# Another order for the first chunks of a fused retention and maxout kernel

## Chip, cores, metric

One core of one Trainium2 chip. The time is device microseconds (us) of one execution; the profile's "span", from the first to the last instruction, is about 1.7 us shorter than the time of the same execution. The engines are PE (TensorE matmul; PEld its weight loads), DVE (VectorE), ACT (ScalarE), POOL (GpSimd) and SP (SyncE, which here only issues DMAs).

## The reference

```python
# q, k, v: (8 batches, 8 heads, 576, 64) float32; moe_w1..3: 512x768; moe_w_out: 768x512
def _attn_ref(q, k, v):
    scores = matmul(q, k.T) / sqrt(64)
    gamma = 1 - 2.0 ** (-5 - arange(8))                      # one per head
    ret = scores * where(rel >= 0, gamma ** rel, 0)          # rel = row - column, causal decay
    return matmul(ret, v)

def _moe_ref(x, w1, w2, w3, w_out):                          # x: 4608 x 512
    return maximum(maximum(x @ w1, x @ w2), x @ w3) @ w_out

x = attn.transpose(0, 2, 1, 3).reshape(4608, 512)            # tokens by heads*head_dim
```

## The kernel before

The 4608 tokens are worked in 36 chunks of 128 rows, four chunks to a tile of 512, nine tiles. A chunk of attention is: two groups of transposes (kT, qT), scores, DVE's masked scores `st`, values `o` from the chunk itself plus the part from the running state ("old state"), then DVE scales `o` into `xT`, the input of the feed-forward part. The state is kept by DVE (`keep`), from chunk to chunk, and scaled by GpSimd.

The weights arrive as float64 bits. DVE and ACT turn each 128x512 block into float32 in four steps of `convert`: expo, frac (two steps), then mant, then expo again and `w`. The feed-forward part of a tile runs while the next tile's attention is done piecewise in between. Only the first chunks ("the head") have nothing to run beside; they are what the change reorders. Tile 0 uses plain matmuls ("up", "down"); later tiles use a seven-product scheme (x, y, z, S, T in the profile).

```python
P, C = 128, 128; CPT = 4                    # chunks per tile
ps_r = tile_pool(bufs=4, space=PSUM)        # tag "r": scores; o from tile 1 on
ps_x = tile_pool(bufs=2, space=PSUM)        # tag "x"
ps_y = tile_pool(bufs=2, space=PSUM)        # tag "y"
opool = tile_pool(bufs=2)                   # output blocks "osb" on their way to memory
# ... cut

def transposes(g):                          # ... cut
    for n, src in (("k", raws["k", g]), ("q", raws.pop(("q", g)))):
        pool, tag = (ps_r, "r") if g > CPT else (ps_x, "x")
        pt = pool.tile([P, NP, C], FP32, tag=tag, name=n + "t")
        for p in range(NP):
            nc.tensor.transpose(pt[:, p, :], pair(src, p), ident[:C, :C])
        t = both[n] = att.tile([P, NP, C], FP32, tag=n + "T", name=n + "T", bufs=2 if n == "k" else 3)
        nc.scalar.copy(t[:], pt[:])

def scores(g):
    s = [ps_r.tile([C, NP, C], FP32, tag="r", name=f"s{j}") for j in range(2)]
    # ... cut: 16 matmuls of kT and qT
    for j in range(2):
        nc.vector.tensor_tensor(st[:, j], s[j][:], mask, op=ALU.mult)

def state(g):
    kr = raws["k", g]
    if begins(g):
        r = start_of(g) or 0
        pool, tag = (ps_r, "r") if g >= CPT else (ps_x, "x")
        kvs[g] = pool.tile([P, NP, D], FP32, tag=tag, name="kv")
        # ... cut: 8 matmuls of k and vd

def keep(g):
    kv = kvs.pop(g)
    # ... cut: first chunk of a batch
    nc.vector.tensor_tensor(t[:], kv[:], states[g][:], op=ALU.add)
    nc.gpsimd.tensor_tensor(t[:], t[:], gs[:], op=ALU.mult)

def values(chunks, new_states=()):
    t, i = divmod(chunks[0], CPT)
    pool, tag = (ps_r, "r") if t > 0 else (ps_y, "y")
    # ... cut: o from st and vd
    for g in new_states:
        state(g)
    # ... cut: old state: o += states[g] x qT
    # ... cut: two DVE products o * gq into xT
    for g in new_states[:1]:
        keep(g)

def decay_values(g):                        # GpSimd: vd = v * decay
    ...

def downs_plain(t, h):                      # tile 0, ... cut
    osb = opool.tile([P, DM], FP32, tag="osb", name="osb")
    nc.scalar.copy(osb[:], b[:])
    nc.sync.dma_start(out[...], osb[:])     # same queue as all loads of q, k, v and weights

decay_values(0); transposes(0); warm(2)     # warm: matmuls of the identity, result unused
decay_values(1); scores(0); transposes(1); scores(1)
decay_values(2); values([0], [0]); transposes(2); scores(2)
values([1], [1]); decay_values(3); transposes(3); scores(3)
convert(2); values([2], [2]); convert(2); transposes(4)
decay_values(4); convert(2); values([3], [3]); convert(4)
# then, per tile: feed-forward steps with the next tile's attention between them
```

## Time and profile before

| | before |
|---|---|
| time, median of 3 | 800.32 us (800.2 to 800.5) |
| span of the profiled execution | 797.9 us, mean clock 1.000 |
| PE idle in the whole span | 797.9 - 785.7 = 12.2 us |
| PE idle before the first "up" (at 30.59) | 7.84 us |

These are stretches of the kernel before; the columns are start and end, length, busy time of PE, PEld, DVE, ACT and POOL (with instructions), PE's clock, the DMA share and GB/s:

```profile
10.00:20.00 10.00, 8.31 (x128) 6.81 (x128) 4.46 (x10) 2.06 (x4) 2.09 (x2) 1.00 1.02 240
20.00:31.00 11.00, 7.59 (x125) 6.21 (x126) 8.24 (x17) 6.17 (x10) 3.90 (x4) 1.00 0.87 218
31.00:120.00 89.00, 89.00 (x428) 44.81 (x430) 78.36 (x141) 50.80 (x77) 7.45 (x7) 1.00 0.67 161
```

PE has idle time in the head and none from 31 to 120 us. The clock is 1.00 in all three. (The first 10 us have 7.26 us busy.)

### The profile page before, as it was taken

Reading aid. Unit: us, or ns where it says so; the run is one execution under the profiler, and the core shown is the slowest. Engines: PE = TensorE matmul, PEld = TensorE weight load, DVE = VectorE, ACT = ScalarE, POOL = GpSimd, SP = SyncE. Lnnn points to the kernel's source line nnn. Section 1 sums busy time; section 2 is a strip of 40 time slices with the busy share of each in tenths; the row PEclk is TensorE's granted clock in tenths of the full one; section 3 lists DMA queues with packets and bytes.
Section 4 is the critical chain, followed back from the end, with each engine's and each line's share of the span. In section 5 each row is a group of like instructions: output and inputs, shape, how many; then the busy total and the mean of one; then the engine's idle time right before and its main releaser. Section 6 shows DMA issues by size and latency. Waiting matters only on the chain. (4 is left out here: it accounts for less than half of the span.)

```text
span 797.9 us, 13707 instructions
## 1 busy us (share of the span) xinstructions
PE 785.7 (98%) x5128; PEld 642.9 (81%) x5128; DVE 414.4 (52%) x833; ACT 174.2 (22%) x401; POOL 139.5 (17%) x158
## 2 busy tenths in 40 slices
PE   7899999999999999999999999999999999999998
PEld 6545546888888888888888888888888888888887
DVE  2897978664354634363535344544545343642341
ACT  2664642111111102111111111111111111111211
POOL 2210108421210130112211121112111201110000
PEclk9999999999999999999999999999999999999999
DMA  9995644333333332332233333333333333001001
GB/s 216 230 226 123 155 108 102 57 57 57 87 57 57 58 78 55 68 58 61 61 55 57 67 82 57 57 57 89 56 55 58 80 62 59 1 14 40 1 1 53
DMA packets 237506, 59.27 MB, mean 74 GB/s; under 512 B 218240, under 2 KB 236160, under 8 KB 237440
## 3 DMA queue, kind: packets, MB, share of 16 engines
q1 hardware_dynamic: 236176, 58.01, 33.5%
q8 instruction: 40, 0.66, 0.3%
q10 hardware_dynamic: 1264, 0.40, 0.2%
q14 instruction: 26, 0.21, 0.1%
HBM read 48.89 MB, written 9.44 MB: 73 GB/s over the span
## 5 line engine op out<-in xcount | busy, mean ns | idle before, releaser
L493 PE MATMUL x<-S,T 128*128 128x256 f32 x576 | 148.1, 380 | 0.7 <-ACT p L498 0.6
L493 PEld LDWEIGHTS x<-S,T 128*128 128x128 f32 x576 | 108.9, 190 | 16.8 <-ACT p L498 1.5
L343 POOL TENSOR_TENSOR H<-h 128x256 f32<-128x256 f32 x24 | 21.0, 874 | 321.2 <-DVE h L536 321.2
L493 PE MATMUL x<-xT,w 128*128 128x256 f32 x288 | 76.1, 387 | 0.0
L493 PE MATMUL x<-S,w 128*128 128x256 f32 x288 | 74.4, 381 | 0.7 <-DVE h L523 0.7
L493 PE MATMUL z<-S,w 128*128 128x256 f32 x288 | 73.9, 379 | 0.0
L493 PE MATMUL y<-xT,w 128*128 128x256 f32 x288 | 73.9, 379 | 0.0
L493 PE MATMUL z<-xT,T 128*128 128x256 f32 x288 | 73.9, 379 | 0.0
L523 DVE TENSOR_TENSOR tmp<-x,p 128x256 f32<-128x256 f32 x48 | 20.4, 425 | 100.0 <-PE x L493 100.0
L498 ACT COPY p<-x 128x256 f32<-128x256 f32 x72 | 26.8, 373 | 192.0 <-PE x L493 192.0
L261 DVE TENSOR_TENSOR xT<-o,gq 128x512 f32<-128x512 f32 (+1 forms) x40 | 23.6, 632 | 83.6 <-PE o L254 83.5
L555 PE MATMUL up<-xT,w 128*128 128x512 f32 x144 | 63.4, 596 | 1.5 <-ACT expo L432 1.5
L493 PEld LDWEIGHTS x<-S,w 128*128 128x128 f32 x288 | 49.4, 189 | 14.2 <-issue 1.3
L493 PEld LDWEIGHTS z<-S,w 128*128 128x128 f32 x288 | 54.7, 190 | 7.4
L493 PEld LDWEIGHTS y<-xT,w 128*128 128x128 f32 x288 | 54.7, 190 | 7.4
L493 PEld LDWEIGHTS x<-xT,w 128*128 128x128 f32 x288 | 53.0, 190 | 9.6 <-issue 1.5
L493 PEld LDWEIGHTS z<-xT,T 128*128 128x128 f32 x288 | 54.3, 189 | 7.9
L555 PEld LDWEIGHTS up<-xT,w 128*128 128x128 f32 x144 | 26.8, 190 | 33.3 <-issue 30.1
L192 DVE TENSOR_TENSOR st<-s,causal 128x512 f32<-128x512 f32 x72 | 45.0, 683 | 16.6 <-PE s L189 15.7
L220 POOL TENSOR_TENSOR state<-state,gs 128x256 f32<-128x256 f32 x24 | 20.1, 836 | 187.5 <-DVE state L219 187.5
L498 ACT COPY u<-x 128x256 f32<-128x256 f32 x72 | 26.8, 372 | 100.0 <-PE x L493 88.9
L161 POOL TENSOR_TENSOR vd<-vraw,gk 128x512 f32<-128x512 f32 x36 | 38.1, 1059 | 56.8 <-DMA vraw<-in_v_dram 56.8
(92 smaller groups left out, 1083.9 us busy)
## 6 DMA issues: line engine op xcount, KB each, us to landing
out_dram<-osb SPq DMA_DIRECT2D x35, 256.0 KB, 2.1
kraw<-in_k_dram SPq DMA_DIRECT2D x32, 256.0 KB, 3.1
vraw<-in_v_dram SPq DMA_DIRECT2D x32, 256.0 KB, 3.5
qraw<-in_q_dram SPq DMA_DIRECT2D x464, 16.0 KB, 1.9
kxraw<-in_k_dram SPq DMA_DIRECT2D x464, 16.0 KB, 1.9
bits<-in_moe_w_dram SPq DMA_DIRECT2D x18, 256.0 KB, 4.5
bits<-in_moe_w_dram SPq DMA_DIRECT2D x36, 128.0 KB, 4.2
bits<-in_moe_w_out_dram SPq DMA_DIRECT2D x6, 512.0 KB, 4.8
```

The lines of the kernel that those rows point to most:

```text
L161: nc.gpsimd.tensor_tensor(t[:], raws.pop(("v", g))[:], gk[:].unsqueeze(2).to_broadcast([C, H, D]), op=ALU.mult)
L192: nc.vector.tensor_tensor(st[:, j], s[j][:], masks[start_of(g)][:].unsqueeze(1).to_broadcast([C, NP, C]), op=ALU.mult)
L220: nc.gpsimd.tensor_tensor(t[:], t[:], gs[:], op=ALU.mult)
L261: nc.vector.tensor_tensor(xT[t][:, b::2, i * C:(i + len(chunks)) * C].rearrange("p u (m c) -> p u m c", c=C), o[b][:].rearrange("p m u c - ...
L343: chores.append(lambda: (pool(s3, a11, a21, op=ALU.subtract), pool(s4, a12, s2, op=ALU.subtract)))
L493: nc.tensor.matmul(out[:], lhsT=w[:, d * P:(d + 1) * P], rhs=xS[t][n][:, d, :], start=first and d == 0, stop=d == 1, skip_group_check=True)
L498: nc.scalar.copy(c[:], src[:])
L523: nc.vector.tensor_tensor(c22, x[:], p7[:], op=ALU.add)
L555: nc.tensor.matmul(ps[:], lhsT=w_sb[i, fb][:, dc * P:(dc + 1) * P], rhs=xT[t][:, dc, :], start=(dc == 0), stop=(dc == NDC - 1))
```

## The change

The intent: fewer waits of PE in the head. The copy of qT is hidden behind other work, kv no longer shares two banks with the transposes, and the first weight's steps move ahead of chunk 3's masks. (The `o` of chunk 3 moves to the group of four banks as well.)

```diff
@@ state
-            pool, tag = (ps_r, "r") if g >= CPT else (ps_x, "x")
-            kvs[g] = pool.tile([P, NP, D], FP32, tag=tag, name="kv")
+            kvs[g] = ps_r.tile([P, NP, D], FP32, tag="r", name="kv")
@@ values
-        pool, tag = (ps_r, "r") if t > 0 else (ps_y, "y")
+        pool, tag = (ps_r, "r") if chunks[0] >= CPT - 1 else (ps_y, "y")
@@ the head
     warm(2)
-    decay_values(1)
     scores(0)
     transposes(1)
+    decay_values(1)
+    values([0], [0])
     scores(1)
+    transposes(2)
     decay_values(2)
-    values([0], [0])
-    transposes(2)
+    values([1], [1])
+    transposes(3)
+    decay_values(3)
     scores(2)
-    values([1], [1])
-    decay_values(3)
-    transposes(3)
+    convert(2)
     scores(3)
-    convert(2)
+    convert(4)
     values([2], [2])
-    convert(2)
-    transposes(4)
     decay_values(4)
     convert(2)
     values([3], [3])
-    convert(4)
+    transposes(4)
+    convert(2)
```

## The prediction

> **What bounds the kernel now.** I read the page first (busy shares, slices), then the stretches of the first 80 us, then the order of work on the matmul engine (PE) and on VectorE (DVE) in the first 31 us, then the landings of the first weights.
>
> ```profile
> PE 785.7 (98%) x5128; PEld 642.9 (81%) x5128; DVE 414.4 (52%) x833; ACT 174.2 (22%) x401; POOL 139.5 (17%) x158
> ...
> 20.00:25.00 5.00, 3.74 (x68) 3.23 (x68) 2.40 (x6) 2.09 (x4) 1.73 (x2) 1.00 0.89 205
> 25.00:30.00 5.00, 3.44 (x64) 2.68 (x56) 4.84 (x9) 3.11 (x6) 2.17 (x2) 1.00 0.82 217
> ...
> 40.00:50.00 10.00, 10.00 (x31) 4.87 (x30) 9.93 (x19) 6.47 (x11) 1.04 (x1) 1.00 0.96 239
> ```
>
> In the stretches the columns are the length, then the busy time of PE, PE's weight loads, DVE, ACT and POOL, the clock, and the DMA share. PE is idle for 797.9 - 785.7 = 12.2 us of the whole span. Adding up the stretches, 7.8 us of that lies before 31 us; from 31 to 120 us PE is never idle. The change edits only what is issued before the first "up" product of the feed-forward part, so its whole worth is how much earlier that product starts. Whatever starts it earlier passes to the end, because behind it PE is full. More than about 6 us cannot be had.
>
> PE's order of time shows the start of "up" and the waits before it; the square brackets hold idle time and what ended it:
>
> ```profile
> 14.78 0.66 PE L179 MATMUL qt<-ident,qraw 128*128 128x128 f32 x4 [0.29 <-DVE state L217]
> 16.12 1.16 PE L189 MATMUL s<-qT,kT 64*128 64x128 f32 x16 [0.68 <-ACT qT L181]
> ...
> 26.36 0.63 PE L179 MATMUL qt<-ident,qraw 128*128 128x128 f32 x4 [0.64 <-PE kt L179]
> 26.91 1.09 PE L242 MATMUL o<-st,vd 128*64 128x128 f32 x16
> ...
> 30.59 0.67 PE L555 MATMUL up<-xT,w 128*128 128x512 f32 x1 [1.52 <-ACT expo L432]
> ```
>
> Three kinds of wait are seen. The q transposes wait for a PSUM bank (0.29 + 0.64 + 0.64 = 1.6 us): kt, qt and kv share two banks, and a kv frees its bank only when DVE has kept the state. The scores wait for the copy of qT just before them (0.64 + 0.67 + 0.68 + 0.67 = 2.7 us). The "up" waits 1.5 us; its releaser is named wrongly, since the ACT operation of L432 ended at 30.53 but is not an input. The real one is in DVE's order of time:
>
> ```profile
> 23.08 1.29 DVE L192 TENSOR_TENSOR st<-s,causal 128x512 f32<-128x512 f32 x2 [2.60 <-PE s L189]
> 24.29 0.42 DVE L429 TENSOR_SCALAR expo<-bits 128x512 int32<-128x512 int32 x1
> 24.62 0.42 DVE L434 TENSOR_SCALAR frac<-bits 128x512 int32<-128x512 int32 x1
> 25.17 0.75 DVE L261 TENSOR_TENSOR xT<-o,gq 128x256 f32<-128x256 f32 x2
> 25.84 0.41 DVE L219 TENSOR_TENSOR state<-kv,state 128x256 f32<-128x256 f32 x1
> 26.17 0.68 DVE L440 SCALAR_TENSOR_TENSOR mant<-frac,mant 128x512 f32<-128x512 int32 x1
> 26.77 1.22 DVE L445 SCALAR_TENSOR_TENSOR expo<-bits,expo 128x512 int32<-128x512 int32 x1
> 28.02 1.42 DVE L451 TENSOR_TENSOR w<-mant,expo 128x512 f32<-128x512 f32 x1
> 29.36 0.41 DVE L429 TENSOR_SCALAR expo<-bits 128x512 int32<-128x512 int32 x1
> 29.70 0.41 DVE L434 TENSOR_SCALAR frac<-bits 128x512 int32<-128x512 int32 x1
> 30.03 0.74 DVE L261 TENSOR_TENSOR xT<-o,gq 128x256 f32<-128x256 f32 x2
> ```
>
> The xT at 30.03 is chunk 3's; "up" starts 0.56 us after it, when its first half is written. From 23.08 on DVE has no gap, so at the end of the head DVE is the bound, while it stood idle 2.16, 2.58, 0.80 and 2.60 us between 10 and 23 us. Each operation follows the next at these distances: masked scores 1.21 for both, expo 0.34, frac 0.34, xT 0.67, state 0.33, mant 0.60, expo 0.72, w 0.62 when undisturbed.
>
> **What the skill says.** "Perfetto Trace Analysis", Identifying the Most-Contended Engine, warns that matmul busy time is no measure of the distance to the roofline; agreed, so I use PE's gaps and not its 98%. The same page, Matmuls, has independent matmul groups rotate through different banks so that evacuation overlaps; the bank waits above are the case where that fails. "SBUF — State Buffer", SBUF: two separate sides, says that a DVE operation with two SBUF inputs and a GpSimd operation lock each other out for a whole instruction; the trace agrees, expo (L445) takes 1.22 us and w (L451) 1.42 us beside GpSimd operations at 26.34 and 27.82, and about 0.69 elsewhere. "TensorE: Matmul & The Clock Gate", What's actually happening, says that an idle window of about 3.4 us halves the array's clock; the trace shows slow starts only (four transposes took 1.06 us at 4.16 and 0.63 at 9.05), and no gap in the head comes near that length.
>
> **The change part by part.** No instruction is added or removed; on every engine the order is new. PE's work per piece, as distances in the trace: transposes 0.43 each for k and q when nothing waits, scores 1.09, values 0.92, kv 0.57, old state 0.60.
>
> (1) Waits of PE removed. With kv in the other four banks, the transposes no longer wait for DVE's state. With other work between a chunk's transposes and its scores, the copy of qT is hidden, except for chunk 0. Up to 1.6 + 2.0 = 3.6 us of PE waiting goes. Laid out from 9.05 on: transposes 1 until 10.43, values 0 at 10.45, scores 1 at 11.95, transposes 2 at 13.05 (k and q of chunk 2 landed at 12.0 and 12.9 by their issue plus time to landing). DVE masks chunk 1 until 14.4, so values 1 at 14.5 to 16.6, transposes 3 until 17.45 (q of chunk 3 lands at 16.9), scores 2 at 17.46, scores 3 at 18.55 to 19.65. The second scores are over 3.4 us earlier than before.
>
> (2) The first weight's bits. They are three loads, the last issued at 16.57 and 3.6 us in flight, so complete near 20.2. DVE masks chunk 2 from 18.65 to 19.94 and must then do the weight's expo and frac before chunk 3's masks, because it runs in order. It cannot start before 20.2. So DVE's dense stretch begins at about 20.2.
>
> (3) DVE from there, by the distances above: expo and frac 0.68, masks of chunk 3 1.21, mant, expo, w 1.94, second weight's expo and frac 0.68. That is 4.5 us: chunk 2's xT at about 24.7, against 25.17 before. After it come xT 0.67, state 0.33, mant 0.60, expo 1.25 (beside GpSimd's state product, as before), w 0.62 to 1.35, then chunk 3's xT: 3.5 to 4.2 us later, at 28.2 to 28.9. Before, 4.86 us lay between the two xT. The reason is that second weight's expo and frac are now ahead, and perhaps that w now runs ahead of GpSimd's vd, whose v lands at 27.7, rather than beside it.
>
> (4) PE at the end. Values 2 follow at 20.0 to 22.1, values 3 begin at 22.2, and their old-state part waits for the state of chunk 2, through DVE and GpSimd: ready about 2.3 us after that xT, at 27.0. This is a new wait of some 3.2 us on PE. Then the old state 0.60, transposes of chunk 4 0.9 and ACT's copy of kT (about 0.6), which frees the bank that "up" takes: 28.95. So "up" starts at the later of 28.95 and xT + 0.56 = 28.8 to 29.45. I take 29.2, against 30.59: **1.4 us gained**, and PE's waiting is mostly moved, not removed.
>
> (5) Afterwards. The second weight is ready before "up" starts, so DVE is about 3 us further on. Before, the third to sixth weights were ready 2.5 to 3.9 us before use; now the lead is larger even if their loads bind. PE stays full, so the 1.4 us reaches the end: 800.32 - 1.4 = 798.9, rounded to 799.0.
>
> **Rivals.** First, PE's removed waits count in full: 3.6 us and more, 796.7. For it, the waits are plainly in the trace; against it, DVE is dense before "up" and the first weight lands at 20.2. Second, the new wait of 3.2 us, or a somewhat longer one, makes the array's clock fall; "up" then runs slowly for some microseconds and takes back 1 to 2 us: 800 to 801. Against it, the gap is just under the page's window. Third, the first weight's load comes late and holds back chunk 3's masks, which it didn't before; each microsecond of lateness costs one: 799.5 to 801. The 16 DMA engines have a share of 0.89 to 1.13 in these stretches, so their order hardly gives a surprise. Fourth, w meets vd as before and "up" starts at 29.45: 799.2.
>
> **Range and chances.** Fourth and main cases span 798.7 to 799.3; the first pulls to below 798, second and third to 801. The run-to-run spread is 0.3 us. So 797.5 to 800.7. Two per cent is 16 us, and only 6.2 us of waiting stand before "up": faster or slower by that much would need something quite outside this.
>
> **What would show each step right or wrong.** The first "up" near 29.2 (28.7 to 29.6); no wait of q transposes for a state, and under 1 us in all for qT; first weight's expo at 20.2 and not waiting much longer; PE's largest gap ahead of the old state of chunk 3, about 3 us; from "up" on PE full and each piece at its old duration. If "up" starts at 28 or sooner, DVE was not the bound that I took it for; if "up" is at 29.2 but its matmuls take longer than 0.59 us per record, the clock fell; if the end doesn't move by what "up" moved, a later stage took it back.

## More of the kernel before

After tile 0's down products, tile 1's "x" products begin at 127.64. In PE's order of time:

```profile
134.54 1.13 PE L493 MATMUL x<-S,w 128*128 128x256 f32 x4 [0.74 <-DVE h L523]
```

This stage takes 134.54 - 127.64 = 6.90 us and has waits on DVE in it. It is not full.

## The result and the profile after

The changed kernel took 799.47 us (median of 6, 799.29 to 800.55), the kernel before 800.16 (median of 6, 799.57 to 800.5). The ratio is 0.9995, with a 95% interval of 0.9982 to 1.0008. No difference is shown at this size. The profiled execution has a span of 797.8 us and a mean clock of 0.996.

The page's busy times of the changed kernel, then its stretches:

```profile
PE 787.3 (99%) x5128; PEld 645.1 (81%) x5128; DVE 415.1 (52%) x833; ACT 174.0 (22%) x401; POOL 139.7 (18%) x158
```
```profile
10.00:20.00 10.00, 10.00 (x145) 8.80 (x145) 4.85 (x11) 3.32 (x6) 3.29 (x4) 0.94 1.04 252
20.00:31.00 11.00, 7.90 (x117) 6.38 (x114) 10.93 (x22) 5.54 (x9) 3.32 (x4) 0.88 0.88 217
31.00:120.00 89.00, 89.00 (x420) 44.62 (x418) 76.53 (x137) 50.31 (x76) 7.10 (x7) 1.00 0.64 161
```

PE is busy without a gap from 10 to 20 us, so the small waits are gone. DVE is full from 20 to 31 us (10.93 of 11). The clock is below 1 in both stretches, and was not before. In the first of them it is a fall that came before the reordered work: chunk 0's scores, at 7.71, took 2.01 us instead of 1.16, with the clock at 0.50 from 8 to 11 us. PE's order up to these scores is the same in both kernels, so this fall is not shown to come of the change. PE is busy 1.6 us more than before with the same 5128 matmuls.

With 6.84 us busy in the first 10 us, this gives an exact account of the start of "up". Before: 7.84 us idle plus 22.75 busy make 30.59. After: 6.26 idle plus 23.90 busy make 30.16. PE's idle time fell by 1.58 us, and the same work took 1.15 us longer, at a lower clock. The sum says where PE's time went, not what "up" waited for. That is in DVE's order of time, of the changed kernel:

```profile
20.95 0.42 DVE L428 TENSOR_SCALAR expo<-bits 128x512 int32<-128x512 int32 x1
21.62 1.29 DVE L192 TENSOR_TENSOR st<-s,causal 128x512 f32<-128x512 f32 x2
...
25.42 0.75 DVE L260 TENSOR_TENSOR xT<-o,gq 128x256 f32<-128x256 f32 x2
...
28.27 1.42 DVE L450 TENSOR_TENSOR w<-mant,expo 128x512 f32<-128x512 f32 x1
29.60 0.74 DVE L260 TENSOR_TENSOR xT<-o,gq 128x256 f32<-128x256 f32 x2
```

Chunk 2's xT is at 25.42, where it was at 25.17 before. Chunk 3's is at 29.60, before at 30.03. PE's order of time in the changed kernel:

```profile
27.74 0.67 PE L253 MATMUL o<-qT,state 64*64 64x128 f32 x16 [3.01 <-POOL state L219]
28.34 1.12 PE L179 MATMUL kt<-ident,kraw 128*128 128x128 f32 x4
29.24 1.06 PE L179 MATMUL qt<-ident,qraw 128*128 128x128 f32 x4
```
```profile
30.16 7.87 PE L554 MATMUL up<-xT,w 128*128 128x512 f32 x16
37.96 1.16 PE L189 MATMUL s<-qT,kT 64*128 64x128 f32 x16
...
134.88 1.13 PE L492 MATMUL x<-S,w 128*128 128x256 f32 x4 [1.08 <-DVE h L522]
```

There is one new wait, 3.01 us long, for GpSimd's state. The transposes behind it take 1.12 and 1.06 us, where undisturbed ones take 0.60 to 0.66. The first two up products take 37.96 - 30.16 = 7.80 us, where they took 37.62 - 30.59 = 7.03 before. The clock of these stretches in the changed kernel:

```profile
28.00:30.00 2.00, 2.00 (x24) 1.73 (x16) 1.97 (x4) 0.51 (x1) 1.13 (x1) 0.58 0.92 239
30.00:32.00 2.00, 2.00 (x5) 0.97 (x4) 2.00 (x6) 1.73 (x4) 0.84 (x1) 0.57 1.00 259
```

In the kernel before the clock is 1.00 in both. So "up" starts 0.43 us sooner, and the scores behind it start 0.34 us later. The 0.34 us is carried unchanged: the first x product of tile 1 is at 127.98 (before 127.64), and the x<-S,w at 134.88 (before 134.54). At 722 us it is given back: before had a wait of 0.3 us there, the changed kernel has none (its x<-S,T is at 723.88, before at 723.84). Before's wait is likely behind an output store, the slowest of which took 4.3 us to land there, against 3.6 us in the changed kernel; the profile of before names PE and not the store. The two spans end 0.1 us apart.

### The profile page after: what moved, and what is told of

Its sections match the earlier page's. It is cut to its first block, busy times and chain, and to the rows that moved or that the text cites. A ratio compares the mean times of both kernels' runs of the same rounds, so it can differ in the third digit from the quotient of the medians.

```text
span 797.8 us, 13706 instructions
## 1 busy us (share of the span) xinstructions
PE 787.3 (99%) x5128; PEld 645.1 (81%) x5128; DVE 415.1 (52%) x833; ACT 174.0 (22%) x401; POOL 139.7 (18%) x158
## 4 chain that ended last, share of the span: by engine, by line
PE 96%; issue 1%; ACTq 1%; ACT 1%; DMA 0%; SPq 0%; POOL 0%; DVE 0%; DVEq 0%; POOLq 0%
PE x L492 31%; PE z L492 15%; PE dx L364 11%; PE up L554 8%; PE y L492 8%; PE dz L364 5%; PE s L189 4%; PE o L241 4%; PE dy L364 3%; PE down L543 2%; PE o L253 2%; PE kv L208 2%; PE kt L179 0%; PE qt L179 0%; ACTq L602 0%
```

## The experiments

All edits are to the changed kernel unless said otherwise. The three groups (e1 to e4, e5 to e8, e9 to e12) ran on three chips, each beside its own runs of the kernel before. "s(4)" is the start of chunk 4's scores, right behind the first two up products.

| run | median us (before on the same chip) | ratio, 95% | "up" | s(4) | x to x<-S,w | executions with clock under 1.000 |
|---|---|---|---|---|---|---|
| before | 800.16 | - | 30.59 | 37.62 | 6.90 | 9 of 33 (beside the experiments) |
| changed | 799.47 (800.16) | 0.9995, 0.9982-1.0008 | 30.16 | 37.96 | 6.90 | 4 of 6 |
| e1 again | 800.61 (799.83) | 1.0003, 0.9985-1.0021 | 30.89 | 38.99 | 6.90 | 5 of 5 |
| e2 gap filled | 801.07 (799.83) | 1.0012, 0.9996-1.0029 | 29.52 | 36.59 | 10.73 | 5 of 5 |
| e3 transposes 4 sooner | 800.72 (799.83) | 1.0010, 0.9989-1.0032 | 30.03 | 38.72 | 6.90 | 5 of 6 |
| e4 second weight later | 799.20 (799.83) | 0.9987, 0.9969-1.0005 | 28.58 | 36.19 | 6.90 | 3 of 5 |
| e5 four output buffers | 800.65 (800.22) | 0.9995, 0.9983-1.0007 | 31.02 | 39.14 | 6.90 | 3 of 5 |
| e6 before, kv's bank only | 801.26 (800.22) | 1.0008, 0.9991-1.0025 | 29.88 | 36.91 | 7.24 | 4 of 6 |
| e7 masks first | 799.58 (800.22) | 0.9993, 0.9981-1.0005 | 29.00 | 37.76 | 6.89 | 5 of 6 |
| e8 masks first, second weight later, four buffers | 796.78 (800.22) | 0.9956, 0.9943-0.9969 | 26.97 | 34.70 | 6.90 | 3 of 5 |
| e9 gap filled, four buffers | 798.83 (800.66) | 0.9975, 0.9957-0.9993 | 30.28 | 37.31 | 6.92 | 1 of 6 |
| e10 as e8, two buffers | 800.92 (800.66) | 1.0001, 0.9981-1.0020 | 27.61 | 35.47 | 9.42 | 5 of 6 |
| e11 before, second weight later | 800.34 (800.66) | 0.9996, 0.9978-1.0015 | 30.07 | 37.66 | 6.90 | 2 of 6 |
| e12 again, once more | 800.44 (800.66) | 0.9997, 0.9978-1.0016 | 31.48 | 39.55 | 6.90 | 6 of 6 |

The starts come from one profiled execution each, the times from 5 or 6. My theory after the result: DVE's chain in program order sets the start of "up", the third part of the change (weights ahead of masks) makes that chain longer, and the new wait on PE lets the clock fall. Rivals: that the banks or the transposes hold "up"; that the fall is nothing but chance; that a later stage takes the gain back.

### e1 and e12: the changed kernel again

No edit.

> The changed kernel itself, unaltered, for the clock. Theory A (the long gap of PE ahead of chunk 3's old-state products lets the array's clock fall, and this takes back what up's earlier start gives): executions with a granted clock of 1.000 have spans near 797.5 us, those at 0.995 about 1 us more, and the kernel before stays at 1.000 in all or nearly all of its executions. Rival (the clock falls at random at the start, whatever the kernel): the kernel before shows clocks under 1.000 just as often. The gain in the mean is 0.3 to 0.8 us either way.

> The changed kernel itself on the chip of these runs, to compare with. Span 797.5 to 799.2, clock under 1.000 in most executions, ratio to the kernel before 0.999 to 1.001; up at 30.0 to 31.0 us, depending on when the first weight's bits land.

Measured: ratios 1.0003 and 0.9997. 15 of 17 executions of the changed kernel have a mean clock below 1.000; before has 9 of 33, which is fewer, but more than I expected of it. The two at 1.000 have spans of 797.6 and 797.7 us. The first expo, at 20.95 in the first profile, is at 21.67 in e1 and at 22.27 in e12. In e1 DVE waited for the weight's bits. From its order of time in e1:

```profile
21.67 0.43 DVE L428 TENSOR_SCALAR expo<-bits 128x512 int32<-128x512 int32 x1 [1.42 <-DMA bits<-in_moe_w_dram]
```

"up" then starts at 30.89 and 31.48, later than before's 30.59. In e12 DVE's own wait for the bits is only 0.30 us, because chunk 2's masks before it were late too (20.68 instead of 19.75): the clock was at 0.50 from 10 to 13 us, and chunk 0's values took 1.80 us instead of 1.09. But the bits landed late as well. ACT's first step needs the same bits, and shows when they were there: at 22.25 in e12, and in the first profile at 20.67:

```profile
20.67 0.78 ACT L429 ACTIVATE mant<-bits,one 128x512 f32<-128x512 uint32 x1 [1.32 <-DMA bits<-in_moe_w_dram]
```

It follows that the gain of 0.43 us in the first profile is not even steady, and that in this order the head's length hangs on when the bits land. In the other runs with the first weight ahead of the masks its expo varied too: 20.81 (e2), 20.81 (e3), 20.91 (e4), 21.81 (e5), 21.06 (e9). In all of these but e2 it started within 0.02 us of ACT's step, that is with the bits.

### e2 and e9: fill the new gap

In e2 unused matmuls of the identity are put before the old-state part of chunk 3. In e9 the same with four output buffers.

```diff
         for g in new_states:
             state(g)
+        if chunks == [CPT - 1]:
+            warm(12, ps_x, "x")        # 24 matmuls in the trace
 # ... cut: warm takes a pool and a tag
-    opool = ... tile_pool(name="opool", bufs=2)     # e9 only
+    opool = ... tile_pool(name="opool", bufs=4)     # e9 only
```

> The changed kernel with 12 idle products of 128x128 (some 2.6 us of PE) put between chunk 3's kv and its old-state products, that is into PE's 3 us gap. Theory A: the clock in 25 to 35 us is 1.00, the transposes of chunk 4 take 0.9 us in all, two up products take 7.0 us rather than 7.8, up still starts near 30.1 (DVE sets it), and the span is 0.5 to 1.0 us shorter than the changed kernel's dipped executions. Rival (the dip has nothing to do with the gap): clock and span as in the changed kernel. Rival (PE's order itself sets up's start): up later by up to 2.6 us.

> The changed kernel with PE's gap filled by 12 idle products, as in the run before, and with four output buffers, so that the late store near 127 us cannot hide the outcome. Theory A (the gap lets the clock fall, and that takes back up's gain): clock 1.00 from 25 to 35 us, the first two up products take 7.0 us in all (7.8 to 8.2 in the changed kernel), clock 1.000 in most executions, span 796.5 to 797.5, 1 us or more below the changed kernel on the same chip. Rival (the clock doesn't count): the same time as the changed kernel within 0.3 us.

Measured in e2: the two up products take 7.07 us instead of 7.80, so the clock held, and s(4) is at 36.59, 1.37 us ahead of the changed kernel. Yet the time is 801.07. The loss is at 127 us. From the orders of time of e2: the output store on SP's queue, ACT's copies into the output block, and PE's matmul that waits:

```profile
127.02 5.17 SPq L550 DMA_DIRECT2D out_dram<-osb  x4
```
```profile
130.62 1.22 ACT L549 COPY osb<-down 128x512 f32<-128x512 f32 x2 [4.95 <-DMA out_dram<-osb]
```
```profile
132.16 2.08 PE L494 MATMUL x<-S,T 128*128 128x256 f32 x4 [3.67 <-ACT p L499]
```

ACT copied the first finished down product at 124.23, but its store was issued only at 127.02, because loads of q, k and v stood before it in the same queue (the last, of v, at 126.40). With two output buffers ACT's third copy waits for that store, PE waits 3.67 us behind ACT, and the matmul after the wait takes 2.08 us instead of 1.03. The stage takes 10.73 us instead of 6.90.

Measured in e9, where four buffers remove that wait: stage 6.92 us, time 798.83, against 800.44 for the unfilled e12 on the same chip; 1 of 6 executions with the clock below 1, against 6 of 6. The filling of e9, in PE's order of time, and a stretch of e9:

```profile
24.56 2.94 PE L113 MATMUL warm<-ident 128*128 128x128 f32 x24
```
```profile
30.00:32.00 2.00, 1.72 (x4) 0.87 (x5) 2.00 (x5) 1.69 (x4) 0.84 (x1) 1.00 0.80 236
```

And the same two places of e12, unfilled:

```profile
29.06 0.67 PE L253 MATMUL o<-qT,state 64*64 64x128 f32 x16 [3.22 <-POOL state L219]
```
```profile
30.00:32.00 2.00, 1.72 (x8) 1.30 (x7) 2.00 (x5) 1.35 (x3) 0.46 (x1) 0.54 0.83 247
```

The clock is 1.00 against 0.54 in these two us. e9 differs from e12 in two edits, but in e5 below the four buffers alone leave the fall: its two up products take 8.12 us. So with the gap open they take 7.80 (first profile), 8.10 (e1), 8.12 (e5) and 8.07 us (e12), with the gap filled 7.07 (e2) and 7.03 us (e9). The open gap is what lets the clock fall here. The kept traces, read from end to end in steps of 5 us, bear this out: among the 14 profiles the clock is below 1 between 25 and 35 us in the first of the changed kernel, e1, e3, e5, e7 and e12, and in no other.

### e3: chunk 4's transposes into the gap

```diff
     values([2], [2])
+    transposes(4)
     decay_values(4)
     convert(2)
     values([3], [3])
-    transposes(4)
     convert(2)
```

> The changed kernel with chunk 4's transposes moved back ahead of chunk 3's values, as before the change. Theory A with DVE as the bound: up starts at the same 30.1 us, within 0.2, since chunk 3's xT follows the second weight's product on DVE; PE's gap shrinks from 3.0 to some 2.1 us, so the clock falls less often; the span falls by 0 to 0.7. Rival (the bank that up takes, freed by the copy of kT of chunk 4, sets up's start): up starts 0.5 us or more earlier.

Measured: "up" at 30.03, 0.13 us sooner than in the first profile of the changed kernel. So the transposes do not hold it, and PE waits 1.76 us for chunk 3's xT there. The clock still fell (the up products take 8.69 us): the gap has become three, of 1.7, 0.5 and 1.8 us. Real work moved into the gap doesn't help where it only leaves a gap behind itself.

### e4: the second weight's steps behind chunk 3's xT

```diff
     scores(3)
-    convert(4)
+    convert(2)
     values([2], [2])
     decay_values(4)
-    convert(2)
     values([3], [3])
     transposes(4)
-    convert(2)
+    convert(6)
```

> The changed kernel with all steps of the second weight moved behind chunk 3's xT. Theory (DVE's order sets up's start): chunk 2's xT comes 0.7 us sooner, chunk 3's xT no longer waits for the second weight's product, and up starts at 28.3 to 29.0, more than 1 us before 30.16, then bound by chunk 4's transposes and their copy; the second weight is still ready within 3.4 us of up's start, so no new wait there over 0.5 us; span 796.2 to 797.2. Rival (PE's chain or the bank sets it): up within 0.3 us of 30.1 and span as the changed kernel's. Rival (the second weight comes too late): up starts sooner, but the second up product waits for the weight by as much.

Measured: "up" at 28.58, 1.58 us sooner than the changed kernel, with the same operations on every engine. The profile names a wait of 0.28 us of the second up product for its weight, the two products take 7.61 us, and s(4) is at 36.19, 1.43 us ahead of before. The profiled execution is at clock 1.000 with a span of 796.1. The time, 799.20, is 0.6 us below before, and the interval includes 1: three of five executions had a fall. That the conversion ahead of chunk 3's xT sets "up" in the changed kernel is confirmed: moving the second weight's steps alone (on DVE, with their parts on ACT) moved it. With them away, the profile names ACT's copy of kT, which frees the bank, as what released "up".

### e7: the masks ahead of the first weight, as before

```diff
     scores(2)
-    convert(2)
     scores(3)
-    convert(4)
+    convert(2)
     values([2], [2])
+    convert(2)
     decay_values(4)
     convert(2)
     values([3], [3])
     transposes(4)
-    convert(2)
+    convert(4)
```

> The changed kernel with one part of the change undone: the weights' steps stand among the masks and chunk 2's values as in the kernel before (chunk 3's masks first). If DVE's in-order queue is what sets up's start and the first weight's steps ahead of the masks are what costs: DVE does chunk 3's masks at 20.2 to 21.5, chunk 2's xT near 22.5 (25.4 in the changed kernel), PE's gap before the old-state products falls from 3 us to under 1.5, up starts at 27 to 27.8 and the clock stays up; span 795.3 to 797 where the stage at 127 us takes little. Rival (the weights' steps placed ahead are a gain): up at 30 or later.

Measured: chunk 2's xT is at 23.08 instead of 25.42, "up" at 29.00 instead of 30.16. So the third part of the change costs 1.2 us at "up" against the first profile of the changed kernel, and 1.9 and 2.5 us against e1 and e12; the other parts gain 1.6 us (30.59 to 29.00). These are differences of single profiles. In the order of e7 late bits cost nothing: they landed at 21.78 here, by ACT's first step, and DVE came from the masks to the expo at 21.96 without a wait. Here "up" starts 0.93 us after its xT (28.07), not 0.56: the profile names the copy of kT as its releaser. The transposes before it ran at full speed and began at 26.00, but on ACT the copy (28.38 to 28.94) stands behind the second weight's two expo steps, which waited 2.41 us for DVE's expo and ran from 26.99 on. So here the order on ACT sets "up", which I had not expected; "up" at 27 to 27.8 and a clock that stays up were both missed. In this run PE's gaps are 0.87 and 1.90 us, with transposes and old state between them, and the clock fell all the same: the two up products take 8.76 us, and s(4) is at 37.76, later than before. The time is 799.58 (before 800.22), within the interval of no change.

### e8 and e10: e7 and e4 together, with four output buffers and with two

```diff
     scores(2)
-    convert(2)
     scores(3)
-    convert(4)
+    convert(2)
     values([2], [2])
     decay_values(4)
     convert(2)
     values([3], [3])
     transposes(4)
-    convert(2)
+    convert(6)
-    opool = ... tile_pool(name="opool", bufs=2)     # e8 only
+    opool = ... tile_pool(name="opool", bufs=4)     # e8 only
```

> What the theories together advise: the changed kernel's banks and order on PE, chunk 3's masks first, the second weight's steps all behind chunk 3's xT, four output buffers. Expected: chunk 3's xT at 25.6 to 26.3 us, up at 26.2 to 27 (bound by chunk 4's transposes and the copy of kT), the second weight within 0.6 us of its use, clock 1.00, no wait for the store near 127 us, span 794.5 to 796, mean ratio 0.995 to 0.998 of the kernel before. If up is no earlier than in the run with the weights as before, the second weight's place doesn't count; if up is earlier but the span is not, a later stage takes it.

> The best version so far with two output buffers, as in the kernel before. If the store counts as soon as the head is more than about 1 us shorter: PE waits 1.5 to 3.7 us behind ScalarE's copy of p near 126 us, x's last product starts later than 6.9 us after the last down product in place of 6.90, and the span is 0.3 to 2.5 us more than with four buffers. Rival (buffers never count, as they didn't in the changed kernel): same span within 0.3 us.

Measured in e8, DVE first and then PE, in order of time:

```profile
22.72 0.76 DVE L260 TENSOR_TENSOR xT<-o,gq 128x256 f32<-128x256 f32 x2 [0.37 <-PE o L253]
...
26.18 0.75 DVE L260 TENSOR_TENSOR xT<-o,gq 128x256 f32<-128x256 f32 x2
```
```profile
26.97 3.70 PE L554 MATMUL up<-xT,w 128*128 128x512 f32 x8 [0.24 <-DVE xT L260]
```
```profile
131.62 1.13 PE L492 MATMUL x<-S,w 128*128 128x256 f32 x4 [1.56 <-DVE h L522]
```

The two xT are 3.46 us apart, not 4.18, since w runs in 0.69 us and no second weight stands between. "up" is 3.62 us ahead of before. The first x product is at 124.72, 2.92 us ahead, the x<-S,w also 2.92 ahead, and the span is 3.3 us shorter. The missing 0.7 us between "up" and x is lost in the first two up products (7.73 us instead of 7.03), where the profile names a 0.40 us wait of the second for its weight. The gain at the end is before's wait near 722 us, which e8 doesn't have. "up" starts 0.79 us after its xT, not 0.56, and right behind the copy of kT, which ends at 26.92. So the bank of the transposes likely binds it, as in e4 and e7, though the profile names DVE. The time is 796.78 us: the largest gain, and with e9 the only one whose interval excludes 1. It was compared with before on one chip; with the changed kernel only by way of before.

Measured in e10, the same with two output buffers: "up" at 27.61, the first x product at 125.48 (2.16 us ahead of before), but the stage behind it takes 9.42 us. PE waits 2.28 us there behind ACT's copy, as in e2, and the clock is 0.50 from 131 to 133 us. The time is 800.92 (before 800.66), so nothing is left of the gain. The head of this execution was 0.64 us longer than e8's, since chunk 0's scores ran at a lower clock (1.90 us instead of 1.16). e8 and e10 ran on different chips, and each is compared with before on its own chip.

### e5: four output buffers alone

```diff
-    opool = ... tile_pool(name="opool", bufs=2)
+    opool = ... tile_pool(name="opool", bufs=4)
```

> The changed kernel with four output buffers in place of two; nothing else. Theory B (a part of what the head gives is given back near 127 to 132 us, where ScalarE's third output copy waits for the store of the first, which waits in the SP queue behind small loads, and PE waits for ScalarE): PE's wait at the x product behind ScalarE's copy of p (0.2 us in the changed kernel, up to 3.7 us in the run with the filled gap) is gone, and so is ScalarE's wait for the store; the mean falls by 0.3 to 1 us against the changed kernel. Rival (the store is not what PE waits for): PE's wait there stays. The head's start of up and its clock are as in the changed kernel.

Measured: 800.65, ratio 0.9995. The wait behind ACT is gone, but the wait on DVE's `h` grew to 1.6 us in its place, and the stage takes 6.90 us as before. So 6.90 us is what DVE's sums there allow, and the buffers matter only where the head is short enough, or the store late enough, to run into them. The changed kernel isn't such a case: the later stage took nothing from it.

### e6: kv's bank alone, in the kernel before

```diff
-            pool, tag = (ps_r, "r") if g >= CPT else (ps_x, "x")
-            kvs[g] = pool.tile([P, NP, D], FP32, tag=tag, name="kv")
+            kvs[g] = ps_r.tile([P, NP, D], FP32, tag="r", name="kv")
```

> The kernel before with one part of the change alone: kv takes its bank from the group of four. If the bank waits counted (0.3, 0.6 and 0.6 us on PE before the last masks): the q transposes don't wait, chunk 3's masks start at 21.6 to 22.1 us in place of 23.08, DVE's dense stretch starts as much sooner, and up starts at 29.2 to 29.7, a gain of about 1 us on up's start, which is more than the whole change gave (0.43). Rival (PE waits that don't set the end): up within 0.2 us of 30.59. The clock stays at 1.00, since PE has no long gap; the span falls by 0.5 to 1.4 us, less what the stage at 127 us takes.

Measured: "up" at 29.88 with the two up products at full clock. That is 0.71 us sooner than before, and more than the whole change gave (0.43). The q transposes now follow those of k without a wait (19.17 and 19.67), so the waits there before were for the bank. The stage behind tile 0 gives 0.34 us of it back (7.24 instead of 6.90, a wait of 1.80 behind ACT's copy, and ACT behind an output store, as in e2). The time isn't better (801.26; 1.0008): 4 of 6 executions had the clock below 1, which I hadn't expected. The two that hadn't have spans of 797.4 and 797.1 us, the others have times up to 803.71. Where the clock fell in those is not known, as only one execution is profiled.

### e11: the second weight later, in the kernel before

```diff
     convert(2)
     transposes(4)
     decay_values(4)
-    convert(2)
     values([3], [3])
-    convert(4)
+    convert(6)
```

> The kernel before with nothing changed but the place of the second weight's steps: all behind chunk 3's xT. If DVE's queue alone set up's start: chunk 3's xT comes 0.7 to 1.4 us sooner but not before PE's old-state products end at 29.1, so up at 29.5 to 29.9 (30.59 before), and the second weight is ready just in time (within 0.5 us); span 0.3 to 1 us less than before, and the clock stays up. So the PE order and the banks are needed for the rest of what the best version gives (up at 26.97). Rival (the second weight's place gives all): up at 28 or sooner.

Measured: "up" at 30.07, 0.52 us sooner than before, then lost again: s(4) is at 37.66 (before 37.62), because now the second up product waits for its weight. Ratio 0.9996. The w beside GpSimd's vd stayed at 1.42 us. The one idea alone, without the shorter PE side, only moves a wait.

## Why the prediction was right or wrong

**The number was right and most of the steps were, but the gain it rests on did not come.** 799.0 was predicted, in 797.5 to 800.7; measured 799.47. That is luck more than insight: the range holds the time of the kernel before (800.16) too. With two repeats at ratios of 1.0003 and 0.9997 the true gain is near zero, not 1.4 us.

- **Step 1, PE's waits removed: right.** No transpose waits for a state, and the scores wait for qT only in chunk 0 (1.29 us in the first profile, a little over the "under 1 us in all" that I gave). PE is full from 10 to 20 us.
- **Step 2, the start of DVE's dense stretch: mis-sized.** 20.2 was predicted. In the first profile it is 20.95 and chunk 2's xT 25.42 instead of 24.7, so +0.72. The bits were there at 20.67 and not at 20.2; this is the larger part of the miss. The rest was PE: scores of chunk 0 took 2.01 us instead of 1.16 at a halved clock, and all behind it slid. In e1 it was the bits alone (21.67), the third rival, and in e12 they landed at 22.25. In no profile of this order were they there before 20.67.
- **Step 3, the length of DVE's chain: right in its parts.** 4.5 us predicted to chunk 2's xT, measured 25.42 - 20.95 = 4.47. From there to chunk 3's xT I took 3.94, in a range of 3.5 to 4.2; measured 4.18, since w met GpSimd's vd and took 1.42 us (the fourth rival). So +0.24. The two terms, 0.72 and 0.24, are the whole difference between 29.2 and 30.16.
- **Step 4, the new wait of PE: right in size, wrong in consequence.** 3.2 us predicted; 3.01 to 3.23 measured, released by GpSimd's state as said. I put the second rival aside because "the gap is just under the page's window". It happened: transposes of chunk 4 took 1.82 us instead of 0.87 (hidden, as "up" starts 0.56 us after xT here, as in e1 and e3), the up products 7.80 instead of 7.03. That is the failed step: it costs 0.77 us after "up" and more than takes back the 0.43. Other executions paid more: 8.10 in e1 and 8.07 in e12. In these the gain at "up" had not come at all (step 2).
- **Step 5, everything after "up" passes on: right in the changed kernel** (+0.34 at 37.96, at 127.98 and at 134.88), though "PE stays full" isn't true at 130 us. In shorter heads (e2, e10) that stage took the gain back.
- **Two slips in the working,** without effect on the result: the terms for the bank (27.0, 0.60, 0.9 and 0.6) add up to 29.1, not 28.95, and the DMA share, said to be 0.89 to 1.13, is 0.82 in one of the stretches shown.
- **What I didn't see:** that the third part of the change works against the first two. The weight's steps before chunk 3's masks hold back chunk 2's xT, from it the state, and from that the old-state part of chunk 3. It makes the gap on PE as well as the later xT (e7, e4, e8). Why weights and masks had been placed in the order of before would have been worth asking.

**Skill.** "TensorE: Matmul & The Clock Gate", HAM oscillation, gives as the short form that gaps should not exceed about 3.4 us. The section behind it, A second HAM failure mode: psum-queue depth-cycling, tells of a kernel where micro-idles between groups of matmuls made the clock go back and forth. The prediction used the first and not the second. Here falls came behind gaps shorter than the first names, of 3.0 to 3.2 us, and in e7 behind 0.87 and 1.90 us, which is nearer to the second; but each was one fall and no back and forth, and one gap of 2.17 (e4) or 2.32 us (e6) brought none in the profile.

**What stays open.** Whether the clock follows the length of a gap or the share of busy time: in 25 to 30 us PE is busy 2.26 us in the changed kernel, 1.77 in e1 and 1.78 in e12, all with falls, and 4.20 (e9), 4.72 (e8) and 3.44 (before) without one in the profile; but e4 at 3.11 held and e6 at 2.68 held, while e3 at 2.77 and e7 at 2.70 fell. That gives no threshold. An execution with a mean clock below 1 need not have had this fall: the first profile and e12 had another one before 15 us as well, e2's was at 130 to 140 us, e10's were before 15 us and at 130 to 135 us, and e8's trace has one at 790 to 795 us. So the counts of executions mix several falls, and where unprofiled ones lose clock (before's 9 of 33 among them) isn't seen. Nor is it known why the landing of the loads varies by about 1.6 us, nor why the clock fell before 15 us in three of the 14 profiles.

## What to carry to other kernels

In a head where nothing runs beside it, first find the engine whose program order sets the next stage, and judge each moved piece by what it delays on that engine: here DVE's weight steps ahead of its masks cost 1.2 us or more, most of what the rest of the change had gained, and made the masks wait for a load whose landing varies. A shortened wait on PE is worth having only if what replaces it doesn't gather into one gap, as a fall of the clock cost the next two products 0.8 to 1.7 us. And when a head gets shorter, look at the next stage that is not full (here two output buffers behind a load queue), since it can take everything back.

## What the Trainium skill lacked or had wrong

- "TensorE: Matmul & The Clock Gate", HAM oscillation: the short form (no idle gaps over about 3.4 us) is too generous as a rule to plan by. In all three profiles of the changed kernel the clock fell behind a gap of 3.0 to 3.2 us (mean clock 0.57 and 0.58 in 28 to 32 us of the first), and 15 of its 17 executions had a mean clock below 1, if not all by this fall; gaps of 0.87 and 1.90 us with work between them did so in e7. A fall cost the following two products 0.77 us in the first profile and up to 1.7 us in e7 (8.76 against 7.03 us). The remark on micro-idles in the section behind it gives no length.
- "DMA: Bandwidth & Descriptors", Issuing engines are not separate DMA queues: it says that starting DMAs from several engines saves only sequencer time, usually small. This isn't shown wrong, but here the time on the sequencer was not small: in e2 a store stood behind loads until 127.02 us though its data had been copied from 124.23 to 124.81, and PE waited 3.67 us behind the copy that needed its buffer. That another issuing engine would have helped was not run; four buffers instead of two did (e8 against e10, e9 against e2).
- "SBUF — State Buffer", SBUF: two separate sides: agrees, and no page gives sizes for this mix: w took 1.42 us beside a GpSimd product and 0.69 alone, expo 1.21 and 0.69.
